# Row maxima moved from a PSUM bank into the tile of squares, with smaller edits ahead of the first expert

## The chip, the core and the metric

The program runs on one core of a Trainium2 chip. The core has a matrix engine (TensorE; PE in the rows, PEld for its weight loads), VectorE (DVE), ScalarE (ACT), GpSimd (POOL) and a queue engine, SyncE (SP), that issues the transfers. Each engine takes its own instructions strictly in order and waits on semaphores for the others. The metric is the device time of one execution in microseconds. The kernel before takes 633.98 us, the median of three runs (633.04 to 634.95).

## The reference

The reference chains three parts, all in float32.

Attention with random features, for 2 batches, 8 heads, 576 positions, head size 64 and 128 features:

```
def phi(x):
    proj = np.einsum('bhsd,md->bhsm', x, omega)
    sq = np.sum(x * x, axis=-1, keepdims=True) / 2.0
    h = proj - sq
    h = h - np.max(h, axis=-1, keepdims=True)
    return np.exp(h) / np.sqrt(m)
q_p, k_p = (phi(q_s), phi(k_s))            # q, k times 64 ** -0.25
kv = np.einsum('bhsm,bhsd->bhmd', k_p, v)
num = np.einsum('bhsm,bhmd->bhsd', q_p, kv)
den = np.einsum('bhsm,bhm->bhs', q_p, k_p.sum(2))[..., None] + 1e-06
```

Then the result, 1152 tokens of width 512, goes through a layer that sends each token to the one of 8 experts with the largest logit (two matrix products with a ReLU between, scaled by a softmax weight and a sigmoid). Last comes a layer in which all 4 experts are applied to every token and summed with given weights.

## The kernel before, in words

Every float32 product that matters is made of three passes: an operand is split into a rounded high part (a cast on ScalarE) and a low part (the difference, `split`, L89 to L91), and high times high, high times low and low times high add up in PSUM.

Attention is cut into 18 units: 16 of (kind k or q, batch b, half of the heads hh, pair of positions jp) and two "rest" units (kr, qr) for positions 512 to 575. The loop at L574 is a software pipeline over stages `st`. In the stage of unit `st`: unit st+1 is transposed on TensorE and split by ScalarE (`qTh`) and VectorE (`qTl`) (`stage_a`, L282); k units of stage st-2 are multiplied into `kv` (`kv_part`, L352); q units of st-2 are transposed (L382, "pt<-e") and copied to `qpT` (L385 on ScalarE, L387 on VectorE); q units of st-3 are multiplied with `kvs` (L400, into a bank `pnd`), divided (L403 to L406, `xn`), transposed again (L416, into the same bank) and split to `xh` and `xl` (L427, L428); and unit st is projected (`project`, L300, twelve matmuls) and given its exponentials (`stage_b`, L311), in two halves a = 0, 1. The matmuls and transposes of attention are chained by hand in this order (`pe`, L254), so that TensorE never runs ahead of a matmul that waits. On the other engines the build's scheduler sets the order, from the order of the code and from estimates of its own.

In `stage_b` the largest value of each row is reduced from PSUM (L324) into four words `mx` at the end of `kbank`. That is the one PSUM bank in which `kv` is accumulated too. Two small instructions (L328, L329) subtract the squares and add them again, so that the offset `nb` is rounded as in the reference, and ScalarE's exponentials read `nb`. The squares `sq` come from `squares` (L262): for the first unit on VectorE, for all others on GpSimd as a tree of adds (L274, L278).

After stage 6 `prep_late` (L232) makes constants for the routing: `fold`, `cmask`, `iota`, `iota1`, `rev`, `ue`, `uc`, and it splits the gate weights. `main_expert` (L461) finds the expert of most tokens of a batch from the gate logits; `E0` (L711) then loads that expert's weights by a dynamic index, and its first matrix is split in eight pieces, the lows alternating between GpSimd and VectorE. From there on the experts follow one another with TensorE as the engine that is busy throughout.

Of the kernel before, what the change touches and what calls it, by code (L numbers as in the profile page):

```python
# [23 lines left out]
NE, NE2, FF = 8, 4, 1024  # L24
# [15 lines left out]
def moe_stack(ctx, tc, q, k, v, omega, w_gate, w_ogate, mw1, mw2, dprobs, dw1, dw2, out):  # L40
    nc = tc.nc
    TT, STT, TS = nc.vector.tensor_tensor, nc.vector.scalar_tensor_tensor, nc.vector.tensor_scalar
# [4 lines left out]
    cp = ctx.enter_context(tc.tile_pool(name="cp", bufs=1))  # L47
# [6 lines left out]
    ps_n = ctx.enter_context(tc.tile_pool(name="ps_n", bufs=2, space=PSUM))  # L54
# [6 lines left out]
    ident = cp.tile([128, 128], F32, name="ident")  # L61
# [12 lines left out]
    grm = cp.tile([128, 4, NE], F32, name="grm")  # L74
    fold = cp.tile([128, 32], F32, name="fold")
    cmask = cp.tile([128, 4], F32, name="cmask")
    i32 = cp.tile([128, 32], I32, name="i32")
    iota = cp.tile([128, 32], F32, name="iota")
    iota1 = cp.tile([128, 32], F32, name="iota1")
    rev = cp.tile([128, NE], F32, name="rev")  # L80
    ue = cp.tile([128, 4, NE], F32, name="ue")
    uc = cp.tile([128, 4, NE], F32, name="uc")
# [59 lines left out]
    ap = pool_a.enter_context(tc.tile_pool(name="ap", bufs=2))  # L142
    G = H // 2
# [86 lines left out]
        nc.gpsimd.tensor_scalar(upper, upper, 0.0, None, op0=ALU.is_gt)  # L230

    def prep_late():  # L232
        TT(fold, ident[:, 0:32], ident[:, 32:64], op=ALU.add)
        TT(fold, fold, ident[:, 64:96], op=ALU.add)
        TT(fold, fold, ident[:, 96:128], op=ALU.add)
        nc.vector.tensor_reduce(cmask, ident.rearrange("p (c r) -> p c r", r=32), axis=AX.X, op=ALU.add)
        nc.gpsimd.iota(i32, pattern=[[1, 32]], base=0, channel_multiplier=0)
        nc.vector.tensor_copy(iota, i32)
        TS(iota1, iota, 1.0, None, op0=ALU.add)
        TS(rev, iota[:, 0:NE], -1.0, float(NE), op0=ALU.mult, op1=ALU.add)  # L240
        nc.vector.tensor_copy(ue, iota[:, 0:NE].unsqueeze(1).to_broadcast([128, 4, NE]))
        nc.vector.tensor_copy(uc, iota[:, 0:4].unsqueeze(2).to_broadcast([128, 4, NE]))
        nc.vector.memset(lgr, 0.0)
        split(wgh, wgl, wg)
        ds_ = cp.tile([128, 9], F32, name="ds_")
        nc.vector.tensor_reduce(ds_, dpr, axis=AX.X, op=ALU.add)
        TS(ds_, ds_, 1e-9, None, op0=ALU.add)
        nc.vector.reciprocal(ds_, ds_)
        TT(pb, dpr, ds_.unsqueeze(2).to_broadcast([128, 9, NE2]), op=ALU.mult)

    sq, st_a, st_e = {}, {}, {}
# [10 lines left out]
    def squares(kind, b, hh, eng):  # L262

        src = raw[kind, b, hh] if b < 2 else raw[kind, 2]
        x = src.rearrange("p h j d -> p (h j) d") if b < 2 else src
        n = x.shape[1]
        x2 = ap.tile([128, n, D], F32, tag="x2", name="x2")
        s = ap.tile([128, n], F32, tag="sq" + kind + ("r" if b == 2 else ""), name="sq")
        if eng is nc.vector:
            for h in range(0, n, 4):  # L270
                TT(x2[:, h:h + 4], x[:, h:h + 4], x[:, h:h + 4], op=ALU.mult)
                nc.vector.tensor_reduce(s[:, h:h + 4], x2[:, h:h + 4], axis=AX.X, op=ALU.add)
        else:
# [102 lines left out]
    def stage_cq(u):  # L376

        kind, b, hh, j = u
        e = heads(*u)
        ps = ps_t.tile([128, G, 128], F32, tag="pt", name="pt")  # L380
        for i in range(G):
            pe(nc.tensor.transpose(ps[:, i, :], e[i], ident))  # L382
        t = ap.tile([128, G, 128], F32, tag="qpT" if b < 2 else f"qpTr{hh}", name="qpT", bufs=4 if b < 2 else 1)
        if j % 2:
            nc.scalar.copy(t, ps)  # L385
        else:
            nc.vector.tensor_copy(t, ps)  # L387
        st_e["T", u] = t
# [185 lines left out]
    for st in range(-1, n + 6):  # L574
# [565 lines left out]
```

## Time and profile before

| what | value |
|---|---|
| median of three runs | 633.98 us |
| profiled execution | 633.71 us, its span 631.9 us, mean granted clock 0.986 |
| busy over the span: TensorE, VectorE, ScalarE, GpSimd | 591.9, 416.7, 257.7, 256.1 us |
| first 115 us: TensorE, VectorE, ScalarE, GpSimd | 84.1, 79.5, 63.7, 49.8 us |
| the other 517 us: TensorE, VectorE | 507.8, 337.2 us |

The page's shares are means over two unlike parts. Attention ends at about 115 us; in it no engine is busy all the time. Behind it TensorE is busy for 98% of the time. So the two parts are to be read apart, the first by who waits for whom, the second by TensorE alone.

### The profile page before, as it was taken

Reading aid. Unit: us, or ns where it says so; the run is one execution under the profiler, and the core shown is the slowest. Engines: PE = TensorE matmul, PEld = TensorE weight load, DVE = VectorE, ACT = ScalarE, POOL = GpSimd, SP = SyncE. Lnnn points to the kernel's source line nnn. Section 1 sums busy time; section 2 is a strip of 40 time slices with the busy share of each in tenths; the row PEclk is TensorE's granted clock in tenths of the full one; section 3 lists DMA queues with packets and bytes.
Section 4 is the critical chain, followed back from the end, with each engine's and each line's share of the span. In section 5 each row is a group of like instructions: output and inputs, shape, how many; then the busy total and the mean of one; then the engine's idle time right before and its main releaser. Section 6 shows DMA issues by size and latency. Waiting matters only on the chain.

```text
span 631.9 us, 11286 instructions
## 1 busy us (share of the span) xinstructions
PE 591.9 (94%) x4302; PEld 538.4 (85%) x4303; DVE 416.7 (66%) x939; ACT 257.7 (41%) x626; POOL 256.1 (41%) x301
## 2 busy tenths in 40 slices
PE   8776685999999999899999999999999999999996
PEld 7656674989978999889899899899898898998995
DVE  7696657688434478976666756667666666666564
ACT  5636556460323154445433343343343343442230
POOL 6983003050000001368646646645745745744220
PEclk9989898999999999899999999999999999999999
DMA  8613106303453302202202102202102101100004
GB/s 220 146 45 88 35 6 219 121 5 105 163 185 135 134 1 68 67 1 67 68 0 68 67 0 68 67 1 67 67 1 66 67 2 67 66 1 2 1 1 149
DMA packets 41241, 42.82 MB, mean 68 GB/s; under 512 B 14816, under 2 KB 29408, under 8 KB 41184
## 3 DMA queue, kind: packets, MB, share of 16 engines
q1 hardware_dynamic: 40896, 42.00, 21.0%
q8 instruction: 35, 0.57, 0.4%
q14 instruction: 22, 0.18, 0.1%
q10 hardware_dynamic: 288, 0.07, 0.0%
HBM read 37.34 MB, written 4.72 MB: 67 GB/s over the span
## 4 chain that ended last, share of the span: by engine, by line
PE 65%; DVE 2%; DMA 1%; issue 0%; ACT 0%; SPq 0%
PE po L634 10%; PE po L635 10%; PE po L636 10%; PE pp L634 9%; PE pp L636 9%; PE pp L635 9%; PE py L634 1%; PE py L636 1%; PE py L635 1%; DMA st<-in_moe_w_dram 1%; PE ph L636 1%; PE ph L635 1%; PE ph L634 1%; DVE wlo L91 1%; DVE xcl L91 0%
## 5 line engine op out<-in xcount | busy, mean ns | idle before, releaser
L91 POOL TENSOR_TENSOR wlo<-st,whi 128x512 fp32r<-128x512 f32 x96 | 116.5, 1235 | 233.5 <-ACT whi L90 228.8
L1085 DVE SCALAR_TENSOR_TENSOR oacc<-po,pb,oacc 128x512 f32<-128x512 f32 x135 | 100.0, 748 | 55.6 <-PE po L636 55.6
L90 ACT CAST whi<-st 128x512 fp32r<-128x512 f32 x120 | 67.8, 592 | 117.6 <-PE po L636 49.2
L634 PE MATMUL po<-whi,hh 128*128 128x512 f32 x288 | 112.4, 390 | 0.0
L635 PE MATMUL po<-wlo,hh 128*128 128x512 f32 x288 | 112.1, 389 | 0.0
L636 PE MATMUL po<-whi,hl 128*128 128x512 f32 x288 | 112.0, 389 | 0.0
L630 POOL TENSOR_TENSOR hl<-c,hh 128x320 fp32r<-128x320 f32 (+1 forms) x64 | 52.6, 822 | 87.4 <-ACT hh L629 74.8
L635 PE MATMUL pp<-xl,whi 128*128 128x320 f32 (+1 forms) x256 | 76.0, 297 | 0.0
L634 PE MATMUL pp<-xh,whi 128*128 128x320 f32 (+1 forms) x256 | 75.9, 297 | 0.0
L636 PE MATMUL pp<-xh,wlo 128*128 128x320 f32 (+1 forms) x256 | 75.9, 297 | 0.0
L636 PEld LDWEIGHTS po<-whi,hl 128*128 128x128 f32 x288 | 54.1, 188 | 11.2
L634 PEld LDWEIGHTS po<-whi,hh 128*128 128x128 f32 x288 | 54.2, 188 | 10.0
L635 PEld LDWEIGHTS po<-wlo,hh 128*128 128x128 f32 x288 | 54.1, 188 | 10.1
L1032 DVE TENSOR_TENSOR c<-u,pp 128x320 f32<-128x320 f32 (+1 forms) x96 | 43.4, 453 | 22.1 <-PE pp L636 21.7
L635 PEld LDWEIGHTS pp<-xl,whi 128*128 128x128 f32 x256 | 48.8, 191 | 1.3
L634 PEld LDWEIGHTS pp<-xh,whi 128*128 128x128 f32 x256 | 48.8, 191 | 1.2
L628 ACT ACTIVATE c<-c 128x320 f32<-128x320 f32 (+1 forms) x64 | 28.5, 445 | 51.7 <-DVE c L1032 50.9
L636 PEld LDWEIGHTS pp<-xh,wlo 128*128 128x128 f32 x256 | 48.8, 191 | 0.0
L625 DVE SCALAR_TENSOR_TENSOR hl<-c,hh 128x320 fp32r<-128x320 f32 (+1 forms) x64 | 45.0, 736 | 0.3
L336 ACT ACTIVATE e<-pj,nb 128x128 f32<-128x128 f32 x144 | 41.2, 378 | 8.2 <-DVE nb L329 8.2
L634 PE MATMUL pp<-xch,whi 128*128 128x320 f32 (+1 forms) x128 | 38.3, 300 | 1.2 <-DVE c L1032 1.2
L634 PE MATMUL ph<-xh,whi 128*128 128x288 f32 x128 | 38.2, 298 | 1.2 <-ACT dg L665 1.2
(265 smaller groups left out, 1335.5 us busy)
## 6 DMA issues: line engine op xcount, KB each, us to landing
st<-in_moe_w_dram SPq DMA_DIRECT2D x32, 512.0 KB, 4.2
st<-in_moe_w_dram SPq DMA_DIRECT2D x10, 1024.0 KB, 6.9
q<-in_q_dram SPq DMA_DIRECT2D x4, 512.0 KB, 4.6
v<-in_v_dram SPq DMA_DIRECT2D x16, 128.0 KB, 4.0
xs<-xn SPq DMA_DIRECT2D x16, 128.0 KB, 1.8
own<-in_moe_w_dram SPq DMA_DIRECT2D x2, 1024.0 KB, 6.7
out_dram<-oacc SPq DMA_DIRECT2D x8, 256.0 KB, 2.0
k<-in_k_dram SPq DMA_DIRECT2D x3, 512.0 KB, 4.0
```

The source lines that it names most:

```text
L90: nc.scalar.copy(hi, src)
L91: eng.tensor_tensor(lo, src, f32(hi), op=ALU.subtract)
L336: nc.scalar.activation(e[:, i // 2, i % 2], ps[:, i // 2, i % 2], AF.Exp, bias=nb[:, i // 2, i % 2:i % 2 + 1])
L625: STT(hl, src, 0.0, f32(hh), op0=ALU.max, op1=ALU.subtract)
L628: nc.scalar.activation(c, c, AF.Relu)
L630: nc.gpsimd.tensor_tensor(hl, c, f32(hh), op=ALU.subtract)
L634: nc.tensor.matmul(ps, sh_, mh, start=start, stop=False)
L635: nc.tensor.matmul(ps, sh_, ml, start=False, stop=False)
L636: nc.tensor.matmul(ps, sl_, mh, start=False, stop=stop)
L1032: TT(c, u, p, op=op)
L1085: STT(oacc[:, T], po, pc, oacc[:, T], op0=ALU.mult, op1=ALU.add)
```

## The change

The words of the maximum, of the square and of the offset now lie next to each other in SBUF: the tile `sq` has four words for each row: 0 minus the maximum, 1 the scaled square, 2 the sum of the two, 3 minus the scaled square. The maximum is reduced straight into word 0 with its sign turned, and two `tensor_reduce` instructions over pairs of neighbouring words give word 2 and then `nb`. `kbank` holds `kv` alone. On GpSimd every `squares` gets two more instructions that write words 1 and 3; on VectorE the first unit's scale is folded into the multiplication and one more reduce writes word 3.

The constants of `prep_late` are written as integers by five `iota` instructions on GpSimd and turned to float32 by one cast; `fold` is one reduce in place of three adds; the low part of the gate weights goes to GpSimd. In the stage loop `main_expert` comes behind the transposes of the q units. All eight lows of E0's first matrix are on GpSimd. The three-pass projection stays as it is.

```
-MXS = 8
...
-    i32 = cp.tile([128, 32], I32, name="i32")
-    iota = cp.tile([128, 32], F32, name="iota")
...
+    i32 = cp.tile([128, 136], I32, name="i32")
+    consts = cp.tile([128, 136], F32, name="consts")
+    iota, iota1, rev = consts[:, 0:32], consts[:, 32:64], consts[:, 64:72]
...
-        TT(fold, ident[:, 0:32], ident[:, 32:64], op=ALU.add)
-        TT(fold, fold, ident[:, 64:96], op=ALU.add)
-        TT(fold, fold, ident[:, 96:128], op=ALU.add)
+        nc.vector.tensor_reduce(fold, ident.rearrange("p (c r) -> p r c", r=32), axis=AX.X, op=ALU.add)
...
-        nc.vector.tensor_copy(iota, i32)
-        TS(iota1, iota, 1.0, None, op0=ALU.add)
-        TS(rev, iota[:, 0:NE], -1.0, float(NE), op0=ALU.mult, op1=ALU.add)
-        nc.vector.tensor_copy(ue, iota[:, 0:NE].unsqueeze(1).to_broadcast([128, 4, NE]))
-        nc.vector.tensor_copy(uc, iota[:, 0:4].unsqueeze(2).to_broadcast([128, 4, NE]))
+        for c, w, pattern, base in ((0, 32, [[1, 32]], 0), (32, 32, [[1, 32]], 1), (64, 8, [[-1, 8]], 8),
+                                    (72, 32, [[0, 4], [1, 8]], 0), (104, 32, [[1, 4], [0, 8]], 0)):
...
+        nc.vector.tensor_copy(consts, i32)
...
-        split(wgh, wgl, wg)
+        split(wgh, wgl, wg, nc.gpsimd)
...
-        s = ap.tile([128, n], F32, tag="sq" + kind + ("r" if b == 2 else ""), name="sq")
+        s = ap.tile([128, n, 4], F32, tag="sq" + kind + ("r" if b == 2 else ""), name="sq")
...
+            nc.vector.tensor_reduce(s[:, :, 3], s[:, :, 1:2], axis=AX.X, op=ALU.add, negate=True)
...
+            for i, f in ((1, hs), (3, -hs)):
+                nc.gpsimd.tensor_scalar(s[:, :, i], s[:, :, 0], f, None, op0=ALU.mult)
...
-        mx = kbank[:, m0:m0 + 4].rearrange("p (x c) -> p x c", x=2)
-        nc.vector.tensor_reduce(mx, ps, axis=AX.X, op=ALU.max)
+        nc.vector.tensor_reduce(s[..., 0], ps, axis=AX.X, op=ALU.max, negate=True)
...
-        STT(mx, s, -hs, mx, op0=ALU.mult, op1=ALU.add)
-        last_nb[0] = STT(nb, s, -hs, mx, op0=ALU.mult, op1=ALU.subtract)
+        nc.vector.tensor_reduce(s[..., 2], s[..., 0:2], axis=AX.X, op=ALU.add)
+        last_nb[0] = nc.vector.tensor_reduce(nb, s[..., 2:4], axis=AX.X, op=ALU.add)
...
-        for b, lg in logits:
-            gate_late[b] = (b, lg) + main_expert(b, lg, ps_n, "nd")
         done, turned = turned, []
...
+        for b, lg in logits:
+            gate_late[b] = (b, lg) + main_expert(b, lg, ps_n, "nd")
...
-    E0.load1(engs=(nc.gpsimd, nc.vector))
+    E0.load1()
```

What the edits do to the order is seen at three places. First TensorE in the stage of unit 12 (q of batch 1): the matmuls into `kv` and into `pnd`, before and then after. A name behind "waits" is the engine whose semaphore is waited for.

```order
L352 MATMUL kv<-v_120,e 64x65 [waits DMAHW7_49,DVE_49]
L352 MATMUL kv<-v_120,e 64x65
L352 MATMUL kv<-v_120,e 64x65 [waits DMAHW0_49]
...
L400 MATMUL pnd<-kvs,qpT 64x65 [waits PE_49]
L400 MATMUL pnd<-kvs,qpT 64x65 x7
L400 MATMUL pnd<-kvs,qpT 64x65 [waits DVE_49]
```

```order
L348 MATMUL kv<-v_116,e 64x65 [waits DMAHW7_49]
L348 MATMUL kv<-v_116,e 64x65
L348 MATMUL kv<-v_116,e 64x65 [waits DMAHW1_49]
...
L396 MATMUL pnd<-kvs,qpT 64x65 [waits DVE_49]
L396 MATMUL pnd<-kvs,qpT 64x65 x7
L396 MATMUL pnd<-kvs,qpT 64x65 [waits DVE_49]
```

The first `kv` matmul no longer waits for VectorE; the first `pnd` matmul, which had only its own engine ahead of it, now does.

Second, VectorE at the same place: the two halves of unit 11, the low part `qTl` of unit 13 and the two `xl` (L428 before, L424 after).

```order
L324 TENSOR_REDUCE kv<-pj 128x4 [waits PE_49]
L328 SCALAR_TENSOR_TENSOR kv<-sq,kv 128x4 [waits DVE_49]
L329 SCALAR_TENSOR_TENSOR nb<-sq,kv 128x4 [waits DVE_49]
L324 TENSOR_REDUCE kv<-pj 128x4 [waits DVE_49,PE_49]
L292 SCALAR_TENSOR_TENSOR qTl<-pt,qTh 128x512 [waits Activation_49]
L328 SCALAR_TENSOR_TENSOR kv<-sq,kv 128x4 [waits DVE_49]
L428 TENSOR_TENSOR xl<-pnd,xh 128x2x128 [waits Activation_49]
L329 SCALAR_TENSOR_TENSOR nb<-sq,kv 128x4 [waits DVE_49]
L428 TENSOR_TENSOR xl<-pnd,xh 128x2x128 [waits Activation_49]
```

```order
L321 TENSOR_REDUCE sq<-pj 128x2x2 [waits PE_49] x2
L324 TENSOR_REDUCE sq<-sq 128x2x2 [waits DVE_49] x2
L291 SCALAR_TENSOR_TENSOR qTl<-pt,qTh 128x512 [waits Activation_49]
L325 TENSOR_REDUCE nb<-sq 128x4 [waits DVE_49] x2
L424 TENSOR_TENSOR xl<-pnd,xh 128x2x128 [waits Activation_49] x2
```

The two maxima now stand next to each other, the small sums behind them, and no `xl` stands between a half's maximum and its `nb`.

Third, VectorE at unit 2, the rest of k, whose squares come from GpSimd (Pool).

```order
L292 SCALAR_TENSOR_TENSOR qTl<-pt,qTh 128x512 [waits Activation_49]
L328 SCALAR_TENSOR_TENSOR kv<-sq,kv 128x4 [waits DVE_49]
L329 SCALAR_TENSOR_TENSOR nb<-sq,kv 128x4 [waits DVE_49]
L324 TENSOR_REDUCE kv<-pj 128x4 [waits DVE_49,PE_49]
L328 SCALAR_TENSOR_TENSOR kv<-sq,kv 128x4 [waits DVE_49,Pool_49]
L329 SCALAR_TENSOR_TENSOR nb<-sq,kv 128x4 [waits DVE_49]
```

```order
L321 TENSOR_REDUCE sq<-pj 128x4 [waits PE_49,Pool_49]
L291 SCALAR_TENSOR_TENSOR qTl<-pt,qTh 128x512 [waits Activation_49]
L324 TENSOR_REDUCE sq<-sq 128x4 [waits DVE_49]
L321 TENSOR_REDUCE sq<-pj 128x4 [waits PE_49]
L325 TENSOR_REDUCE nb<-sq 128x4 [waits DVE_49]
```

The wait for GpSimd has moved from the small sum to the maximum itself, which writes the tile that GpSimd fills, and the low part `qTl` of the next unit, which stood ahead of it, now stands behind it.

## Rows read from the trace of the kernel before

**Rows 1.** Windows: stretch, then each engine's busy time, granted clock, DMA share, GB/s.
```profile
0.00:115.00 115.00, 84.11 (x979) 74.08 (x981) 79.48 (x231) 63.73 (x198) 49.81 (x85) 0.94 0.42 114
115.00:632.00 517.00, 507.78 (x3326) 464.33 (x3324) 337.21 (x709) 193.96 (x429) 206.26 (x216) 1.00 0.17 58
```

**Rows 2.** Waits of TensorE in 0 to 115: total us, times, longest.
```profile
PE kv L352 <- DVE nb L329: 14.0, 8, 2.3
PE pnd L416 <- DVE xn L406: 7.3, 3, 4.3
PE pt L382 <- DVE qTl L292: 4.5, 4, 1.3
```

**Rows 3.** Timeline of TensorE, unit 11 to unit 12: start, us, instruction [idle before].
```profile
65.41 0.39 PE L306 MATMUL pj<-omh,qTh 128*128 128x256 f32 x1
...
70.10 1.15 PE L352 MATMUL kv<-v,e 128*64 128x65 f32 x32 [2.13 <-DVE nb L329]
...
72.77 0.58 PE L306 MATMUL pj<-omh,qTh 128*128 128x256 f32 x1
```

**Rows 4.** Timeline of VectorE in the same stage.
```profile
66.55 0.69 DVE L324 TENSOR_REDUCE kv<-pj 128x4 f32<-128x512 f32 x1
...
69.56 0.42 DVE L428 TENSOR_TENSOR xl<-pnd,xh 128x256 fp32r<-128x256 f32 x1 [0.46 <-ACT xh L427]
69.90 0.15 DVE L329 SCALAR_TENSOR_TENSOR nb<-sq,kv 128x4 f32<-128x4 f32 x1
69.96 0.42 DVE L428 TENSOR_TENSOR xl<-pnd,xh 128x256 fp32r<-128x256 f32 x1
```

**Rows 5.** Groups by shape, 0 to 160: count, busy us, mean ns, idle before.
```profile
L324 DVE TENSOR_REDUCE kv<-pj 128x4 f32<-128x512 f32 x36 | 25.1, 696 | 11.0 <-PE pj L308 7.1 <-ACT kvs L373 1.9 <-PE pnd L416 0.5
L292 DVE SCALAR_TENSOR_TENSOR qTl<-pt,qTh 128x512 fp32r<-128x512 f32 x18 | 12.3, 685 | 1.7 <-ACT qTh L291 1.7
L91 POOL TENSOR_TENSOR wlo<-st,whi 128x512 fp32r<-128x512 f32 x8 | 11.4, 1431 | 44.6 <-ACT whi L90 44.6
L328 DVE SCALAR_TENSOR_TENSOR kv<-sq,kv 128x4 f32<-128x4 f32 x36 | 5.8, 160 | 1.5 <-POOL sq L278 0.6
```

**Rows 6.** Timeline of VectorE while the late constants are made.
```profile
32.20 0.45 DVE L233 TENSOR_TENSOR fold<-ident 128x32 f32<-128x32 f32 x1
32.57 0.27 DVE L236 TENSOR_REDUCE cmask<-ident 128x4 f32<-128x128 f32 x1
...
34.87 1.87 DVE L241 COPY ue<-iota 128x32 f32<-128x32 f32 x1
...
37.36 1.02 DVE L247 TENSOR_SCALAR ds__581<-ds__581 128x9 f32<-128x9 f32 x1
...
39.28 0.74 DVE L406 TENSOR_TENSOR xn<-pnd,rd 128x256 f32<-128x256 f32 x2
```

**Rows 7.** Timeline of TensorE: what waits for that, and two matmuls behind lows.
```profile
39.74 0.77 PE L416 MATMUL pnd<-ident,xn 128*128 128x128 f32 x4 [4.33 <-DVE xn L406]
...
104.56 0.44 PE L416 MATMUL pnd<-ident,xn 128*128 128x128 f32 x2 [1.74 <-DVE xn L406]
106.23 0.69 PE L416 MATMUL pnd<-ident,xn 128*128 128x128 f32 x2 [1.23 <-DVE xn L406]
```

**Rows 8.** Timeline of GpSimd and VectorE at unit 2.
```profile
15.34 0.19 POOL L278 TENSOR_TENSOR sq<-x 128x8 f32<-128x8 f32 x1
...
15.57 0.17 DVE L328 SCALAR_TENSOR_TENSOR kv<-sq,kv 128x4 f32<-128x4 f32 x1 [0.57 <-POOL sq L278]
```

**Rows 9.** Timeline of TensorE: the first two waits for nb.
```profile
17.18 1.15 PE L352 MATMUL kv<-v,e 128*64 128x65 f32 x32 [1.04 <-DVE nb L329]
...
21.69 1.15 PE L352 MATMUL kv<-v,e 128*64 128x65 f32 x32 [0.86 <-DVE nb L329]
```

**Rows 10.** Windows in which the granted clock is low, columns as in Rows 1.
```profile
72.00:75.00 3.00, 3.00 (x27) 2.88 (x24) 2.07 (x7) 0.00 (x0) 0.00 (x0) 0.55 0.25 86
...
102.00:113.00 11.00, 5.75 (x70) 4.84 (x70) 7.88 (x18) 7.19 (x19) 5.49 (x4) 0.69 0.62 191
```

More of the change, by code (lines that the diff above doesn't have):

```diff
@@ L76, in moe_stack @@
     cmask = cp.tile([128, 4], F32, name="cmask")
-    i32 = cp.tile([128, 32], I32, name="i32")
-    iota = cp.tile([128, 32], F32, name="iota")
[L79 to L82, printed above, removed]
+    i32 = cp.tile([128, 136], I32, name="i32")
+    consts = cp.tile([128, 136], F32, name="consts")
+    iota, iota1, rev = consts[:, 0:32], consts[:, 32:64], consts[:, 64:72]
+    ue, uc = (consts[:, c:c + 32].rearrange("p (c e) -> p c e", e=NE) for c in (72, 104))
     lgr = cp.tile([16, 128], F32, name="lgr")
@@ L232, in prep_late @@
     def prep_late():
-        TT(fold, ident[:, 0:32], ident[:, 32:64], op=ALU.add)
-        TT(fold, fold, ident[:, 64:96], op=ALU.add)
-        TT(fold, fold, ident[:, 96:128], op=ALU.add)
+        nc.vector.tensor_reduce(fold, ident.rearrange("p (c r) -> p r c", r=32), axis=AX.X, op=ALU.add)
         nc.vector.tensor_reduce(cmask, ident.rearrange("p (c r) -> p c r", r=32), axis=AX.X, op=ALU.add)
-        nc.gpsimd.iota(i32, pattern=[[1, 32]], base=0, channel_multiplier=0)
-        nc.vector.tensor_copy(iota, i32)
-        TS(iota1, iota, 1.0, None, op0=ALU.add)
-        TS(rev, iota[:, 0:NE], -1.0, float(NE), op0=ALU.mult, op1=ALU.add)
-        nc.vector.tensor_copy(ue, iota[:, 0:NE].unsqueeze(1).to_broadcast([128, 4, NE]))
-        nc.vector.tensor_copy(uc, iota[:, 0:4].unsqueeze(2).to_broadcast([128, 4, NE]))
+        for c, w, pattern, base in ((0, 32, [[1, 32]], 0), (32, 32, [[1, 32]], 1), (64, 8, [[-1, 8]], 8),
+                                    (72, 32, [[0, 4], [1, 8]], 0), (104, 32, [[1, 4], [0, 8]], 0)):
+            dst = i32[:, c:c + w]
+            nc.gpsimd.iota(dst if len(pattern) == 1 else dst.rearrange("p (a b) -> p a b", b=8),
+                           pattern=pattern, base=base, channel_multiplier=0)
+        nc.vector.tensor_copy(consts, i32)
         nc.vector.memset(lgr, 0.0)
-        split(wgh, wgl, wg)
+        split(wgh, wgl, wg, nc.gpsimd)
         ds_ = cp.tile([128, 9], F32, name="ds_")
@@ L267, in squares @@
         x2 = ap.tile([128, n, D], F32, tag="x2", name="x2")
-        s = ap.tile([128, n], F32, tag="sq" + kind + ("r" if b == 2 else ""), name="sq")
+        s = ap.tile([128, n, 4], F32, tag="sq" + kind + ("r" if b == 2 else ""), name="sq")
+        hs = SCALE * SCALE / 2
         if eng is nc.vector:
             for h in range(0, n, 4):
-                TT(x2[:, h:h + 4], x[:, h:h + 4], x[:, h:h + 4], op=ALU.mult)
-                nc.vector.tensor_reduce(s[:, h:h + 4], x2[:, h:h + 4], axis=AX.X, op=ALU.add)
+                STT(x2[:, h:h + 4], x[:, h:h + 4], hs, x[:, h:h + 4], op0=ALU.mult, op1=ALU.mult)
+                nc.vector.tensor_reduce(s[:, h:h + 4, 1], x2[:, h:h + 4], axis=AX.X, op=ALU.add)
+            nc.vector.tensor_reduce(s[:, :, 3], s[:, :, 1:2], axis=AX.X, op=ALU.add, negate=True)
         else:
@@ L276, in squares @@
             while w:
-                dst = x2[:, :, 0:w] if w > 1 else s.unsqueeze(2)
+                dst = x2[:, :, 0:w] if w > 1 else s[:, :, 0:1]
                 nc.gpsimd.tensor_tensor(dst, x2[:, :, 0:w], x2[:, :, w:2 * w], op=ALU.add)
                 w //= 2
+            for i, f in ((1, hs), (3, -hs)):
+                nc.gpsimd.tensor_scalar(s[:, :, i], s[:, :, 0], f, None, op0=ALU.mult)
         sq[kind, b, hh] = s
@@ L317, in stage_b @@
         if rest:
-            s = sq[kind, 2, 0][:, G * a:G * a + G].rearrange("p (x c) -> p x c", x=2)
+            s = sq[kind, 2, 0][:, G * a:G * a + G].rearrange("p (x b) c -> p x b c", x=2)
         else:
-            s = sq[kind, b, hh].rearrange("p (h j) -> p h j", j=4)[:, 2 * a:2 * a + 2, 2 * jp:2 * jp + 2]
+            s = sq[kind, b, hh].rearrange("p (h j) c -> p h j c", j=4)[:, 2 * a:2 * a + 2, 2 * jp:2 * jp + 2]
         e = ap.tile([128, 2, 2, M], F32, tag="e" if not rest else f"er{kind}{a}", name="e", bufs=EB if not rest else 1)
-        m0 = 512 - 4 * MXS + 4 * (flip[0] % MXS)
-        mx = kbank[:, m0:m0 + 4].rearrange("p (x c) -> p x c", x=2)
-        nc.vector.tensor_reduce(mx, ps, axis=AX.X, op=ALU.max)
+        nc.vector.tensor_reduce(s[..., 0], ps, axis=AX.X, op=ALU.max, negate=True)
         nb = ap.tile([128, 2, 2], F32, tag="nb", name="nb", bufs=4)
-        hs = SCALE * SCALE / 2
-        STT(mx, s, -hs, mx, op0=ALU.mult, op1=ALU.add)
-        last_nb[0] = STT(nb, s, -hs, mx, op0=ALU.mult, op1=ALU.subtract)
+        nc.vector.tensor_reduce(s[..., 2], s[..., 0:2], axis=AX.X, op=ALU.add)
+        last_nb[0] = nc.vector.tensor_reduce(nb, s[..., 2:4], axis=AX.X, op=ALU.add)
         flip[0] += 1
```

## The prediction, made before the changed kernel ran

> **What bounds the kernel now.** I read the windows first: they part the span at 115 us [rows 1]. Behind it TensorE is busy 507.8 of 517 us, and the change touches nothing that it does there, so that part keeps its length and only begins earlier or later. Ahead of it TensorE is busy 84.1 of 115 us and VectorE 79.5; neither is full, so waits between engines set the length, and the rest of the reading is in that stretch.
>
> The waits of TensorE come next [rows 2]. The largest is 14.0 us in eight waits, all of the same kind: a matmul into `kv` waits for VectorE to finish `nb`. It does not need `nb`. What `kv` multiplies are exponentials of two stages ago; the wait exists because `mx` lies in the bank that `kv` is written to. The timeline of one stage shows the price [rows 3, 4]: TensorE has been free since 67.97, VectorE ends the last `nb` at 69.90 + 0.15 = 70.05, the `kv` matmuls start at 70.10, and unit 12 is projected at 72.77, 7.36 us after unit 11. In that stage the last `nb` even stands behind an `xl` that waited for ScalarE.
>
> **The change part by part.** The sum is made against the profiled execution, 633.7 us, of which 631.9 is the span.
>
> *The bank (term 1).* In the order after, no `kv` matmul waits for VectorE. The first two of the eight waits, 1.04 and 0.86 [rows 9], I count at nothing: at unit 2 GpSimd now has two instructions more for the squares, four more `iota` and parts of another unit ahead of them, six or more of about 0.19 [rows 8], so the squares come 1.1 to 1.5 us later. VectorE waited 0.57 for them already, and now waits with the maximum itself, ahead of `qTl`. The six others are 14.0 - 1.9 = 12.1 us. What is late next? In the stage of rows 3, the first `pnd` matmul needs a bank that the `xl` of the stage read. Without the wait `kv` would be done by 67.97 + 1.1 = 69.1. VectorE, from 66.55 on, has two maxima (1.4), sums (0.3), `qTl` (0.69), sums (0.2) and two `xl` (0.8) [rows 4, 5]: about 69.9, against 70.38 before. So the second half of `pnd` starts at 69.9 and not at about 71.2 to 71.6; of the 2.13 some 1.3 is gained and 0.85 is not. Two of the six stages have two such `pnd` (units 12 and 16); in the others one short `pnd` follows, and the first `xl` lies beside `kv`. Term 1 is 12.1 - 2 x 0.85 = **10.4**. Bounds: 3.6 if only VectorE's own shorter chain counts (two halves cost about 2.5 us with their dependent steps before and 1.9 after, 0.6 x 6), 14.0 if nothing comes in its place.
>
> *The sums (term 2).* 72 small scalar_tensor_tensor of 0.16 us become 72 `tensor_reduce` of two words. No row has that shape. The bounds are 0.16 (L328, as many words written [rows 5]) and 0.27 (the reduce of 128 words, L236 [rows 6]). I take 0.16, the row nearest in words, so nothing; at 0.27 they add 72 x 0.11 = 7.9 us of VectorE, of which at most half lies on the chain, 4. The maximum reads the same 512 words of PSUM, 0.70, and only its four results go elsewhere: nothing.
>
> *The late constants (term 3).* Before, VectorE is at them from 32.20 to 39.28 [rows 6], and the transposes of `xn` behind them make TensorE wait 4.33 us [rows 7]. Up to 37.36 that is 5.16 us; in its place stand two reduces at 0.27, one cast of 136 words, a memset and a small reduce (0.3 together). The cast is between 0.16 and the 1.87 of the copy of 32 words. So 2.5 to 4.2 us are saved. I take **4.0**: the copy and the tensor_scalar of 1.02 are long because GpSimd was at work, and the reduce in the same stretch was not [rows 6]. The Trainium skill (SBUF — State Buffer, Who interferes with whom) says that VectorE's copies, casts and tensor_scalar in the two-port modes, and a tensor_tensor with both inputs in SBUF, contend with GpSimd for a port pair that one instruction holds to its end, and that a tensor_reduce never does on trn2; the trace agrees, 1.87 and 1.02 beside 0.27. By that rule the one cast may still meet a long GpSimd instruction, and term 3 would be 2.5.
>
> *E0's lows (term 4).* Four lows leave VectorE. Behind them TensorE waited 1.74 and 1.23 us for `xn` [rows 7], 2.97 together. The granted clock in that stretch was 0.69, with 5.75 us of TensorE busy [rows 10]; at full clock that is 1.8 less. I take a third of it, since ScalarE's casts and the wait for the transfer stay in the same stretch: 2.97 + 0.6 = **3.6**. Bounds 0 and 4.8.
>
> *The clock after the waits (term 5).* From 72 to 75 the granted clock was 0.55 [rows 10]: the lower level, 1.2 GHz, for nearly all of it, behind a TensorE that had waited 2.13 us in the stage before. With the wait shorter, 3.0 x 0.45 = 1.35 may come back; I take **1.2**, bounds 0 and 1.35.
>
> *What it costs (term 6).* In the four stages in which q units are transposed, TensorE waits for `qTl` (4.5 us in four [rows 2]). After, the 0.68 us copy to `qpT` stands ahead of `qTl` on VectorE in these; the adjacent maxima give back some of it. I take 0.5 each, 2.0, and 0.4 for the late squares at the start: **-2.4**, bounds 0 and -5.
>
> *The tail (term 7).* The eight lows in series on GpSimd take 8 x 1.43 = 11.4 us [rows 5] from the landing of the weights on, and the landing hangs on the gate of batch 0, which moves up less than the end of attention does. Before, all eight were done when attention ended. After, TensorE catches up with them, or with unit 17's exponentials behind the casts on ScalarE, for about one low: **-1.3**, bounds 0 and four lows, -5.7. Moving `main_expert` behind the transposes exchanges one short wait for another: nothing. The eight pairs of small GpSimd instructions later on lie where GpSimd is idle: nothing.
>
> Sum: 10.4 + 0 + 4.0 + 3.6 + 1.2 - 2.4 - 1.3 = 15.5 us. 633.7 - 15.5 = 618.2; the median of three lies 0.3 above the profiled execution, so the forecast is **618.5 us**.
>
> **The rivals.**
>
> *The wait comes back in another place.* Attention is a ring of TensorE, VectorE and ScalarE; with the `kv` wait gone, `pnd` waits for `xl`, the transposes for `qTl`, the projection for the exponentials that free its banks, in every stage and not in two. Then term 1 is its lower bound, 3.6, and term 5 goes with it: 3.6 + 4.0 + 3.6 - 2.4 - 1.3 = 7.5, 626.5 us. For it: VectorE is busy 79.5 of 115 us, and the first `pnd` matmul has a new wait for it. Against: in the stage that I followed row by row 1.3 of 2.13 stays.
>
> *Nothing comes in its place.* The losses of terms 1, 6 and 7 (1.9 + 1.7 + 2.4 + 1.3) do not show, since a TensorE that idles less also keeps its clock: 15.5 + 7.3 = 22.8, 611.2 us. Against: VectorE alone would then be busy some 70 of 92 us in a ring with many steps.
>
> *The sums are dear, and it is slower.* Each half has two `tensor_reduce` in a row between its maximum and its exponentials. If one of them costs 0.16 + y, the loss is up to 72 y, as far as all lie on the chain. It passes the gain at y = 15.5 / 72 = 0.22, and is slower by 0.3% at y = 17.4 / 72 = 0.24, a price of 0.40 us: 636 us. The Trainium skill speaks for it (VectorE: DVE Perf Modes, Rules for kernel authors): it calls `tensor_reduce` on a hot path the slowest VectorE operation and advises restructuring. The trace bears that out only for long rows: 0.70 for 512 words against 0.69 for a scalar_tensor_tensor of the same length is level [rows 5], and 128 words took 0.27.
>
> *It does nothing.* Another chain than attention sets when the experts start, 634 us. Against: the first expert's index comes out of attention's last stages, and TensorE is busy with attention until the experts begin.
>
> **How the numbers follow.** Chances: the forecast 0.64, the wait comes back 0.20, nothing in its place 0.09, dear sums 0.04, nothing happens 0.03. Below 0.3%, 1.9 us, a measurement of this kernel can't tell a change from none. All of the first three are faster: 0.93; no change 0.03 and slower 0.04. The range takes in both neighbours: 611 at the low end, and 628 at the high end for the returning wait with the dearer sums and term 3 at 2.5. The forecast's own range is 614 to 623.
>
> **What would show it.** Right: the `kv` wait for `nb` gone from TensorE's waits; attention done near 99 and not at 115; two `xn` waits behind the constants below 1.5 us; no VectorE lows for the first expert; the small reduces at 0.16 to 0.2. Wrong: `pnd` or the transposes waiting more than 8 us in total for `xl` or `qTl`; the granted clock low for longer than before; unit 2's maximum more than 3 us later; TensorE waiting for the first expert's lows.

## The result, and the profile after

The changed kernel takes **614.19 us**, the median of four runs (613.24 to 615.89). The kernel before took 633.51 beside it on the same chip (633.04 to 634.95): a ratio of 0.9694, 95% interval 0.9663 to 0.9725, so 19.3 us less. 618.5 us was forecast, with 614 to 623 as the forecast's own range; the result lies just inside its lower end. The profiled execution took 613.25 us, its span is 611.3 us: 20.6 us less than the span before, against 15.5 in the sum.

The windows of the kernel after, parted where attention ends; columns as in [rows 1]:

```profile
0.00:98.00 98.00, 83.92 (x1003) 74.25 (x1004) 67.97 (x225) 63.12 (x205) 58.47 (x111) 0.98 0.44 118
98.00:611.00 513.00, 504.54 (x3302) 459.75 (x3300) 336.67 (x704) 192.21 (x423) 207.68 (x218) 1.00 0.18 61
```

TensorE is busy 84 of 98 us, the last 3 of them for the first expert already, where it was 84 of 115; and the granted clock there is 0.98 where it was 0.94. The first expert's first matmul starts at 95.02 (before: 115.33), the first matmul of its second matrix at 119.29 (139.47), and 492 us follow in either kernel.

The waits of TensorE up to 98 us (what waited, on what: total us, times, longest), in answer to [rows 2]:

```profile
PE pt L378 <- DVE qTl L291: 2.8, 3, 1.2
PE pt L378 <- DVE qpT L383: 2.7, 3, 0.9
PE pj L307 <- DVE qTl L291: 2.6, 2, 2.4
PE pj L305 <- ACT e L332: 2.2, 2, 1.2
PE pnd L396 <- DVE xl L424: 1.2, 3, 0.4
...
PE pnd L412 <- DVE xn L402: 0.6, 1, 0.6
```

The 14.0 us of `kv` for `nb` are gone, and of the 7.3 for `xn` 0.6 is left. The stage of [rows 3] reads now, in TensorE's timeline:

```profile
59.46 0.39 PE L305 MATMUL pj<-omh,qTh 128*128 128x256 f32 x1
...
61.97 1.15 PE L348 MATMUL kv<-v,e 128*64 128x65 f32 x32
63.54 1.15 PE L396 MATMUL pnd<-kvs,qpT 128*64 128x65 f32 x32 [0.42 <-DVE xl L424]
64.62 0.39 PE L305 MATMUL pj<-omh,qTh 128*128 128x256 f32 x1
```

5.16 us from unit 11 to unit 12 and not 7.36; in place of 2.13 us for `nb`, 0.42 for `xl`. The groups of VectorE up to 98 us, in answer to [rows 5]:

```profile
L321 DVE TENSOR_REDUCE sq<-pj 128x4 f32<-128x512 f32 x36 | 24.2, 689 | 12.8 <-PE pj L307 7.8 <-POOL sq L278 4.6
...
L324 DVE TENSOR_REDUCE sq<-sq 128x4 f32<-128x8 f32 x36 | 5.4, 156 | 0.1
L325 DVE TENSOR_REDUCE nb<-sq 128x4 f32<-128x8 f32 x36 | 5.2, 154 | 0.1
```

The new sums take 0.155 us each, as forecast. The 4.6 us of idle time in the first row are one wait, at unit 2: the maximum now writes into the tile of squares and waits for GpSimd, which finished them late, at 18.15 and not at 15.53 [rows 8]. That maximum in VectorE's timeline, before and then after, and what TensorE then waits for at unit 3, after:

```profile
14.29 0.70 DVE L324 TENSOR_REDUCE kv<-pj 128x4 f32<-128x512 f32 x1
```

```profile
18.19 0.69 DVE L321 TENSOR_REDUCE sq<-pj 128x4 f32<-128x512 f32 x1 [4.62 <-POOL sq L278]
```

```profile
19.53 0.39 PE L307 MATMUL pj<-omh,qTl 128*128 128x256 f32 x1 [2.39 <-DVE qTl L291]
```

Unit 4 is projected at 25.87; before it was 22.78. So the gain was made although the start lost 3.1 us. Two more windows, in answer to [rows 10]:

```profile
22.00:25.90 3.90, 3.90 (x45) 3.50 (x44) 1.78 (x6) 1.79 (x7) 3.36 (x8) 0.58 0.77 250
64.60:69.40 4.80, 4.80 (x81) 4.45 (x77) 4.03 (x14) 2.96 (x11) 0.00 (x0) 1.00 0.19 58
```

The low clock (0.58) now stands at the start, behind TensorE's waits of 2.39 and 1.18 at unit 3; in the stage of unit 12 it is 1.00.

### The profile page after: what moved, and what is told of

The parts are those of the page before. It is cut to its first block, busy times and chain, and to the rows that moved or that the text cites. A ratio compares the mean times of both kernels' runs of the same rounds, so it can differ in the third digit from the quotient of the medians.

```text
span 611.3 us, 11277 instructions
## 1 busy us (share of the span) xinstructions
PE 588.5 (96%) x4302; PEld 534.0 (87%) x4303; DVE 404.6 (66%) x929; ACT 255.3 (42%) x626; POOL 266.2 (44%) x328
## 4 chain that ended last, share of the span: by engine, by line
PE 66%; DVE 3%; DMA 1%; issue 1%; ACT 0%; SPq 0%
PE po L630 11%; PE po L632 11%; PE po L631 11%; PE pp L630 9%; PE pp L632 9%; PE pp L631 9%; PE py L630 1%; PE py L632 1%; PE py L631 1%; DMA st<-in_moe_w_dram 1%; PE ph L631 1%; PE ph L630 1%; PE ph L632 1%; DVE wlo L88 1%; DVE xcl L88 1%
## 5 line engine op out<-in xcount | busy, mean ns | idle before, releaser
L88 POOL TENSOR_TENSOR wlo<-st,whi 128x512 fp32r<-128x512 f32 x100 | 120.6, 1228 | 218.5 <-ACT whi L87 216.7
L332 ACT ACTIVATE e<-pj,nb 128x128 f32<-128x128 f32 x144 | 39.3, 396 | 5.6 <-DVE nb L325 5.5
```

## The experiments

The table has the time at which TensorE starts the first projection of a unit, from the timelines of the profiled executions; "expert" is the first expert's first matmul, "second" the first of its second matrix. The names of the runs are those below. The stage of a unit is here the time from this start to that of the next unit.

| unit | before | after | e1 | e5 | e12 | e6 | e10 |
|---|---|---|---|---|---|---|---|
| 4 | 22.78 | 25.87 | 23.75 | 24.29 | 24.59 | 22.68 | 22.54 |
| 6 | 33.28 | 35.98 | 41.11 | 42.10 | 34.60 | 32.69 | 32.41 |
| 7 | 44.15 | 41.26 | 48.86 | 49.93 | 41.27 | 38.42 | 37.68 |
| 16 | 101.12 | 87.58 | 98.09 | 97.39 | 87.90 | 84.72 | 84.02 |
| 17 | 112.61 | 92.24 | 102.16 | 102.84 | 92.06 | 89.51 | 88.74 |
| expert | 115.33 | 95.02 | 104.2 | 106.3 | 93.9 | 92.3 | 91.5 |
| second | 139.47 | 119.29 | 131.2 | 131.2 | 119.7 | 116.6 | 115.8 |

Ratios are to the kernel before, run beside each; gains in us are differences of these medians. The build's scheduler orders VectorE's instructions anew for every kernel, so a run can differ from its neighbour in more than the lines shown.

### The bank alone (e1)

```
-        m0 = 512 - 4 * MXS + 4 * (flip[0] % MXS)
-        mx = kbank[:, m0:m0 + 4].rearrange("p (x c) -> p x c", x=2)
+        mx = ap.tile([128, 2, 2], F32, tag="mx", name="mx", bufs=8)
```

> The kernel before with one edit: the words of the maxima lie in an SBUF tile of their own instead of the bank of kv; the two scalar_tensor_tensor sums, the constants and the lows of the first expert stay as before. Theory (the shared bank held TensorE): the kv waits for nb, 14.0 us, are gone, and attention ends 11 to 14 us earlier, since the squares are no later than before; 620 to 623 us. Rival (the gain of the change comes from the work that it takes off VectorE, and the wait comes back as pnd and transposes waiting for xl and qTl): 628 us or more.

Measured: 624.26 us, ratio 0.984 (0.9812 to 0.9868), 9.9 us gained, between the two expectations. No `kv` matmul waits for VectorE any more, and from unit 7 to the expert 15.8 us are saved (55.3 for 71.2). But units 4 to 7 cost 25.1 us for 21.4. VectorE's groups up to 105 us show a price that neither side had foreseen:

```profile
L327 DVE SCALAR_TENSOR_TENSOR mx<-sq,mx 128x4 f32<-128x4 f32 x34 | 11.0, 333 | 0.2
L328 DVE SCALAR_TENSOR_TENSOR nb<-sq,mx 128x4 f32<-128x4 f32 x34 | 10.0, 306 | 0.1
```

The same instructions took 160 ns while `mx` lay in PSUM [rows 5]. With `mx` in SBUF the means are 333 and 306, about twice that.

### The form of the sums (e5)

```
-        nc.vector.tensor_reduce(s[..., 2], s[..., 0:2], axis=AX.X, op=ALU.add)
-        last_nb[0] = nc.vector.tensor_reduce(nb, s[..., 2:4], axis=AX.X, op=ALU.add)
+        TT(s[..., 2], s[..., 0], s[..., 1], op=ALU.add)
+        last_nb[0] = TT(nb, s[..., 2], s[..., 3], op=ALU.add)
```

> The changed kernel with its two sums as tensor_tensor adds of the same SBUF words instead of tensor_reduce. Theory (an instruction of VectorE with both inputs in SBUF is held up by GpSimd's squares, a tensor_reduce is not): the adds take 0.3 us or more in the mean and not 0.155, VectorE is busy 10 us longer in attention, unit 7 is projected 3 us later or more; 617 to 622 us. Rival (the form of the sum doesn't matter, and what the bank alone did not give lies in the constants and the lows): 0.16 us in the mean, 613.5 to 615 us.

Measured: 625.81 us, ratio 0.988 (0.985 to 0.991), slower than the upper end expected. In the code only the form of 72 instructions of four words differs from the changed kernel, and 11.1 of its 19.3 us are lost. The scheduler also set some twenty of VectorE's instructions at units 2 to 5 in another order, and what that alone is worth isn't shown. Unit 4 is projected earlier than in the changed kernel; the loss lies behind it. Units 4 to 7 took 25.6 us for 15.4, with VectorE busy 21.3 of them and the granted clock at 0.80 for 1.00. The rows of VectorE, then of GpSimd, in the same stretch (start, duration):

```profile
23.36 1.91 DVE L325 TENSOR_TENSOR nb<-sq 128x4 f32<-128x4 f32 x1
...
27.63 1.64 DVE L324 TENSOR_TENSOR sq<-sq 128x4 f32<-128x4 f32 x1
29.19 0.68 DVE L321 TENSOR_REDUCE sq<-pj 128x4 f32<-128x512 f32 x1
```

```profile
23.35 1.89 POOL L271 TENSOR_TENSOR x<-k 128x1024 f32<-128x1024 f32 x1
25.32 2.07 POOL L275 TENSOR_TENSOR x<-x 128x512 f32<-128x512 f32 x2
27.35 1.89 POOL L271 TENSOR_TENSOR x<-q 128x1024 f32<-128x1024 f32 x1
```

An add of four words that starts beside a GpSimd multiplication ends with it: 23.36 + 1.91 = 25.27 and 23.35 + 1.89 = 25.24; 27.63 + 1.64 = 29.27 and 27.35 + 1.89 = 29.24. Beside two GpSimd instructions of 0.28, from 22.71 on, the adds at 23.04 and 23.16 took 0.20 and 0.17. Up to 110 us 21 adds took more than 0.25, and each of them ended 0.01 to 0.03 us behind the end of a GpSimd instruction. In the changed kernel 32 of the reduces lay wholly within a GpSimd instruction of 0.5 us or more, and the longest of them took 0.17. VectorE's groups up to 105 us have the means, against 156 and 154 ns for the reduces of the changed kernel among the same GpSimd work:

```profile
L325 DVE TENSOR_TENSOR nb<-sq 128x4 f32<-128x4 f32 x34 | 13.1, 396 | 0.1
...
L324 DVE TENSOR_TENSOR sq<-sq 128x4 f32<-128x4 f32 x34 | 10.8, 328 | 0.1
```

The Trainium skill (SBUF — State Buffer, Who interferes with whom) says that a VectorE instruction with two SBUF inputs contends with a GpSimd instruction that reads SBUF, one with at most one SBUF input outside the two-port modes does not, and a tensor_reduce on trn2 never does; the trace agrees in all three: 0.31 to 0.40 with two inputs in SBUF, 0.16 with one of them in PSUM, 0.155 as a reduce.

### The bank back (e2), and the maxima by themselves (e12)

The changed kernel with the maxima in `kbank` and the sums as scalar_tensor_tensor:

```
-        nc.vector.tensor_reduce(s[..., 0], ps, axis=AX.X, op=ALU.max, negate=True)
+        m0 = 480 + 4 * (flip[0] % 8)
+        mx = kbank[:, m0:m0 + 4].rearrange("p (x c) -> p x c", x=2)
+        nc.vector.tensor_reduce(mx, ps, axis=AX.X, op=ALU.max)
...
+        STT(mx, s[..., 1], -1.0, mx, op0=ALU.mult, op1=ALU.add)
+        last_nb[0] = STT(nb, s[..., 1], -1.0, mx, op0=ALU.mult, op1=ALU.subtract)
```

> The changed kernel with the maxima back in words of the kv bank, and the two sums as scalar_tensor_tensor again; squares, constants, main_expert and lows stay as changed. Theory: the kv waits come back, 11 to 13 us, 625 to 627 us; what is left of the gain, 7 to 8 us, is the constants and the lows. Rival (the other edits carry the gain): 618 us or less.

Measured: 628.59 us, ratio 0.9907 (0.9877 to 0.9937): 5.6 us gained of 19.3. The other edits leave a little less than expected.

The opposite: the kernel before with the changed `squares` and `stage_b`, and all else as it was. The lines of the change's diff that it has:

```
+        s = ap.tile([128, n, 4], F32, tag="sq" + kind + ("r" if b == 2 else ""), name="sq")
...
+        nc.vector.tensor_reduce(s[..., 0], ps, axis=AX.X, op=ALU.max, negate=True)
...
+        nc.vector.tensor_reduce(s[..., 2], s[..., 0:2], axis=AX.X, op=ALU.add)
+        last_nb[0] = nc.vector.tensor_reduce(nb, s[..., 2:4], axis=AX.X, op=ALU.add)
```

> The kernel before with the maxima, the squares' four words and the two tensor_reduce sums of the change, and nothing else: old constants, old place of main_expert, lows of the first expert on both engines. Theory (free bank and sums in a form that GpSimd does not hold up carry the whole gain): 611 to 613.5 us, attention done near 92 us. Rival (the lows and the place of main_expert carry a part that the runs so far hide): 616 us or more.

Measured: 613.99 us (609.99 to 614.09, two of six runs near 610), 0.5 above the range expected, ratio 0.9664 (0.9632 to 0.9695): 19.6 us gained, as much as by the whole change. The late constants and the lows of the first expert, 7.6 us of the forecast's 15.5, add nothing to it.

### The late constants (e14 on the kernel before, e6 on the changed one)

On the kernel before, `prep_late` and the tiles of the change, as its diff has them:

```
-        nc.vector.tensor_copy(iota, i32)
...
+        nc.vector.tensor_copy(consts, i32)
...
+        split(wgh, wgl, wg, nc.gpsimd)
```

> The kernel before with the late constants of the change, and nothing else. By term 3 of the prediction 4.0 us are gained in the stage of unit 6: 630 us. Theory from the opposite edit on the changed kernel (which gained 2 us): the stage gains 3 to 5 us, the four more iota instructions hold up the squares of unit 2 by 0.5 to 2 us; 630.5 to 633 us. Rival: no gain in the stage either, 633 to 635 us.

Measured: 631.47 us, ratio 0.9966 (0.9945 to 0.9988), 2.1 us gained. The stage of unit 6 took 6.47 us for 10.87: 4.4 saved, as term 3 has it; 1.3 went in the next stage (7.79 for 6.53) and 0.5 at the start.

On the changed kernel, the old constants, the same lines the other way round:

```
-        nc.vector.tensor_copy(consts, i32)
...
+        nc.vector.tensor_copy(iota, i32)
...
+        split(wgh, wgl, wg)
```

> The changed kernel with the late constants made on VectorE as before. Term 3 of the prediction: 4.0 us are lost, all of them in the stage in which unit 6 is projected (5.28 us long in the changed kernel): 618 to 619 us. Rival (the stage costs more, since its small instructions also meet GpSimd's squares): 5 to 6 us, 619.5 to 620.5 us. Other rival (the wait is taken up later in the ring): 615 us or less.

Measured: 612.13 us, ratio 0.9674 (0.9638 to 0.9709). Nothing is lost; 2.5 us more are gained than by the change, though the intervals overlap. The stage of unit 6 took 5.73 us for the changed kernel's 5.28, and unit 4 came 3.2 us earlier: with four `iota` fewer on GpSimd, VectorE's wait for the squares of unit 2 is 2.6 us and not 4.6. Part of the 3.2 is the clock. The windows from 20 to 26 us, first of the changed kernel and then of this run:

```profile
20.00:26.00 6.00, 4.82 (x50) 4.22 (x49) 3.38 (x12) 3.65 (x13) 5.30 (x10) 0.72 0.55 169
```

```profile
20.00:26.00 6.00, 5.30 (x66) 4.83 (x65) 4.00 (x13) 4.49 (x17) 5.29 (x10) 1.00 0.64 200
```

At a granted clock of 0.72, 4.82 us of TensorE are, by an estimate from this row, 1.3 us more than at 1.00. The old constants, then, had not been long in themselves. GpSimd's row in the kernel before, beside VectorE's copy `ue` in [rows 6]:

```profile
34.80 1.91 POOL L274 TENSOR_TENSOR x<-q 128x1024 f32<-128x1024 f32 x1
```

The copy of 32 words that took 1.87, from 34.87 to 36.74, ended 0.03 us behind that multiplication. With the maxima alone (e12) the same copy and the cast, in VectorE's timeline, fell among GpSimd's short instructions, and only `pb` met a long one:

```profile
33.62 0.23 DVE L241 COPY ue<-iota 128x32 f32<-128x32 f32 x1
...
35.17 1.71 DVE L249 TENSOR_TENSOR pb<-dpr,ds__590 128x36 f32<-128x36 f32 x1
```

```profile
33.56 0.24 POOL L280 TENSOR_TENSOR x<-x 128x32 f32<-128x32 f32 x1
...
34.94 1.89 POOL L276 TENSOR_TENSOR x<-k 128x1024 f32<-128x1024 f32 x1
```

### The lows of the first expert (e7 and e8)

On the kernel before, all eight on GpSimd:

```
-    E0.load1(engs=(nc.gpsimd, nc.vector))
+    E0.load1()
```

> The kernel before with the lows of the first expert all on GpSimd, and nothing else. By term 4 of the prediction 3.6 us are gained, in the stage of unit 16: 630 us. Rival (as in the changed kernel the edit is worth nothing): 633 to 634.5 us. If 630 is measured here and nothing was lost by the opposite edit on the changed kernel, the two gains overlap: the same stage, shortened once.

Measured: 630.03 us, ratio 0.9941 (0.9913 to 0.9969): 3.55 us gained (2.0 to 5.5 by the interval), where term 4 had 3.6, and in its stage (unit 16 to 17 8.11 us for 11.49). The same edit undone on the changed kernel:

```
-    E0.load1()
+    E0.load1(engs=(nc.gpsimd, nc.vector))
```

> The changed kernel with the lows of the first expert alternating between GpSimd and VectorE again. By term 4 of the prediction the two waits for xn come back, 2.5 to 3.6 us, in the stage of unit 16: 616.7 to 618 us. Theory from the run with the bank alone (its stage of unit 16 was short, 4.07 us, with these lows on VectorE, and 2.9 us were lost later): the stage stays under 5.5 us and 2 to 3 us are lost between the first matmul of the first expert and its second matrix; 616 to 617.5 us. Rival (the lows are hidden either way): 613.5 to 615 us.

Measured: 614.54 us, ratio 0.9706 (0.9667 to 0.9745): nothing lost. The stage of unit 16 takes 4.71 us with the lows on VectorE. What changed is VectorE's order there. Before, a low stood ahead of `xn`, and waited 1.67 for ScalarE; in this run, and in the run with the maxima alone, whose rows are shown, the lows stand behind both `xn`:

```profile
102.82 1.35 DVE L91 TENSOR_TENSOR wlo<-st,whi 128x512 fp32r<-128x512 f32 x1 [1.67 <-ACT whi L90]
104.09 0.41 DVE L406 TENSOR_TENSOR xn<-pnd,rd 128x256 f32<-128x256 f32 x1
```

```profile
87.97 0.42 DVE L407 TENSOR_TENSOR xn<-pnd,rd 128x256 f32<-128x256 f32 x1
...
88.70 0.42 DVE L407 TENSOR_TENSOR xn<-pnd,rd 128x256 f32<-128x256 f32 x1
...
91.85 1.54 DVE L91 TENSOR_TENSOR wlo<-st,whi 128x512 fp32r<-128x512 f32 x2
```

The first pair is the kernel before, the second the run with the maxima alone. The weights arrive about 0.5 to 1.1 us after unit 16's projection has begun in both (first cast at 101.64 and 89.02), so it is the order and not the arrival. With the lows on VectorE again the expert starts earlier, at 93.56 and not at 95.02, and takes as much longer to its second matrix, 25.8 us for 24.3: that one comes at 119.38 and 119.29.

### How much room VectorE has (e4)

```
-        nc.vector.tensor_reduce(s[..., 2], s[..., 0:2], axis=AX.X, op=ALU.add)
+        for _ in range(2):
+            nc.vector.tensor_reduce(s[..., 2], s[..., 0:2], axis=AX.X, op=ALU.add)
+        nc.vector.tensor_reduce(nb, s[..., 2:4], axis=AX.X, op=ALU.add)
         last_nb[0] = nc.vector.tensor_reduce(nb, s[..., 2:4], axis=AX.X, op=ALU.add)
```

> The changed kernel with the first of the two sums of every half done twice: 36 more tensor_reduce of 4 words on VectorE, between the maximum and the exponentials. At 0.16 us each that is 5.8 us of VectorE. Theory (VectorE's chain from the projection to the exponentials is part of the ring): at least a third of it shows, 616 to 619 us. Rival (VectorE has slack in every stage): within 1 us of the changed kernel, 614 to 615 us. A third reading, that these reduces are dear (0.27 or more each), would be seen in their rows, and give 620 us or more.

The kernel that ran repeats both sums and not only the first, 72 more reduces and not 36, 11 us of VectorE. Measured: 618.08 us (614.21 to 619.11), ratio 0.9726 (0.9697 to 0.9755), 3.2 us less gained than by the change. The reduces keep their 0.155 us. 3.5 us are lost in the stage of unit 6 alone (8.81 for 5.28), where VectorE now met long GpSimd instructions in two rows of the constants (1.87 and 1.07); the stages of units 7 and 17 lost 1.1 and 1.0, and unit 4 came 0.8 earlier. The nine stages from unit 8 to unit 17 take 46.26 us for 45.92: with the bank free VectorE has room there for the 0.6 us that each of them got.

### The start (e3, e10, e11)

The squares of the k rest on VectorE:

```
+            with tc.issue_after(last_nb[0].ins):
+                return squares(kind, 2, 0, nc.vector)
```

> The changed kernel with the squares of the k rest on VectorE, behind the first unit's offsets, instead of on GpSimd. Theory (the late squares of unit 2 held the start back): VectorE's wait of 4.6 us for them is gone, unit 4 is projected 2.5 to 3.5 us earlier than in the changed kernel, and that stays to the end: 611 to 612 us. Rival (the ring swallows it: another wait, for the next squares on GpSimd or for the transfers of k and q, takes its place): 613.5 to 615 us.

Measured: 612.82 us, ratio 0.9667 (0.9644 to 0.9691), which can't be told from the changed kernel. The wait of 4.6 is gone and unit 4 comes at 22.98, 2.9 earlier; 1.4 is given back in the stage of unit 6 (6.66 for 5.28), where `ds_` and `pb` took 1.38 and 1.09.

Then the constants ahead of the first projection, `pb` behind attention, and GpSimd's squares of the k rest ahead of those of the first q:

```
+    prep_slots()
+    prep_early()
...
+            with tc.issue_after(last_sq["k", 2].ins):
+                squares(kind, b, hh, nc.gpsimd)
...
+        prep_pb()
```

> The changed kernel with three things moved: the constants (and the slot numbers) are made while VectorE and GpSimd wait for the first transfers, the normalised domain weights pb behind attention, and GpSimd does the squares of the k rest ahead of those of the first q, not interleaved with them. Theory (the late squares cost 2.8 us at unit 2, and VectorE's work in the stage of the constants is on the path): VectorE's wait of 4.6 us is gone, unit 4 is projected near 23, unit 7 near 37.5 to 39 and not at 41.26, attention ends 2.5 to 4 us earlier; 610 to 612 us. Rival (the stages before unit 8 are set by the transfers or by GpSimd's other squares): 613 to 615 us.

Measured: **609.65 us** (608.68 to 611.21), ratio 0.9619 (0.9592 to 0.9647), 24.3 us gained, a little more than expected; the interval lies below that of the changed kernel. Units 4 and 7 came where expected. Unit 1, however, was projected at 11.76 and not at 9.50. The last run puts `fold`, `cmask` and the cast behind the second unit's offsets.

```
-    prep_early()
+    prep_iotas()
...
+        if st == 2:
+            with tc.issue_after(last_nb[0].ins):
+                prep_early()
```

> The kernel of the early constants with one thing put elsewhere: fold, cmask and the cast stand behind the second unit's offsets on VectorE, not ahead of the first projection. Theory: unit 1 is projected near 9.5 and not at 11.76, and all later units 1.5 to 2.5 us earlier: 607 to 608.5 us. Rival (the squares of the first q on GpSimd set unit 3, whatever stands ahead): 609 to 610.5 us.

Measured: 610.04 us, ratio 0.9618 (0.9592 to 0.9644), and unit 1 at 11.55: the theory fell. The windows from 6.6 to 11.5 us, first of the changed kernel and then of this run, show where the 2 us are:

```profile
6.60:11.50 4.90, 3.59 (x27) 3.18 (x27) 4.21 (x11) 2.23 (x8) 3.09 (x3) 1.00 1.07 245
```

```profile
6.60:11.50 4.90, 4.38 (x19) 3.98 (x20) 3.58 (x11) 0.44 (x1) 3.73 (x9) 0.65 1.26 264
```

The granted clock is 0.65 where it was 1.00, so a good part of the stretch ran at the lower level, 1.2 GHz. TensorE had waited 0.40 for `qTh`, 0.31 for `oml` and 0.21 for `qTl` ahead of it; in the changed kernel it was 0.40 and 0.22. What brings the clock down here is left open.

## Why the prediction was right in the time and wrong in the parts

By stages of the two profiled executions, the 20.6 us come together as follows; the forecast's terms are sorted into the same places.

| place | forecast | measured |
|---|---|---|
| five stages with a `kv` wait (units 7, 8, 11, 12, 15): terms 1, 5 | 10.2 | 9.7 |
| stage of unit 16: rest of term 1, term 4 | 5.0 | 6.8 |
| stage of unit 6: term 3 | 4.0 | 5.6 |
| other stages from unit 4 on: term 6 | -2.0 | +1.4 |
| start to unit 4: term 6 | -0.4 | -3.1 |
| behind unit 17: term 7 | -1.3 | +0.2 |

That the time came out inside the range is partly luck: the start lost 2.7 us more than forecast, all the other places together gained 7.8 us more, and the two errors cancel in part.

*Term 1, the bank,* was right where it was followed row by row: 33.6 us in the five stages became 23.9. What came in its place was 0.4 and not 0.85, in the two stages with two `pnd` (units 11 and 15 as counted here, 12 and 16 in the prediction). Its bound of 14.0 for "nothing comes in its place" was too low, though: the maxima and sums alone, without the other edits, gain 19.6. This is the step that failed. The prediction took each wait for the property of its own stage and priced it once. But the waits for `xn` at unit 6 and unit 16 were not made by the constants and the lows alone; when the bank is free, VectorE's order and its place beside GpSimd change, and these waits shrink with the constants and the lows as they were: these two stages took 6.67 for 10.87 and 4.16 for 11.49 in that run.

*Terms 3 and 4* were sized well for the kernel before: 4.4 us in its stage (2.1 in the end) and 3.55 us. On top of term 1 they are worth nothing in the end: the new constants still shorten the stage of unit 6 (5.28 for 6.67 with the maxima alone), but unit 4 comes 1.3 us later. Measured one at a time, the maxima with their sums, the constants and the lows make 19.6 + 2.1 + 3.55 = 25.2; together they make 19.3. With the bank shared (e2) the other edits gain 5.6, as much as constants and lows do by themselves; so it is the gain of the free bank that theirs overlaps with.

*Term 2, the sums,* has the right number, 0.155 us, and missed its meaning. Their form is not a detail of equal price: it is what lets the words lie in SBUF. With adds 11.1 us of the gain go. The prediction asked whether GpSimd holds up the cast of term 3, and did not ask it of 72 instructions whose second input moves from PSUM into SBUF. The rival of dear sums leaned on another sentence of the Trainium skill (VectorE: DVE Perf Modes, Rules for kernel authors), that a tensor_reduce on a hot path is the slowest operation; here the measurement differs, and it decides: 0.155 for the reduce and 0.33 to 0.40 for the tensor_tensor in its place. The rows that the prediction set beside that sentence, 0.70 and 0.69 for 512 words, were level too and did not bear it out.

*Term 5* can't be told from term 1 in these stages; the granted clock in the stage of unit 12 is 1.00, against the 0.55 of [rows 10].

*Term 6* erred twice. The start lost 3.1 and not 0.4: the prediction had the squares 1.1 to 1.5 later, and they were 2.6 later. VectorE began unit 2's first maximum at 18.19 and not at 14.29, 3.9 later and so beyond the 3 that the prediction had named as a sign of a wrong step, and everything behind it on VectorE, `qTl` of unit 3 too, came later with it. The four stages in which q units are transposed lost nothing, 19.4 us for 19.8: in three of them TensorE now waits for `qpT` and not for `qTl`, 0.9 each, and in the fourth 1.2 for `qTl`.

*Term 7* was -0.1: 24.3 us from the expert's first matmul to its second matrix, 24.1 before.

*The rivals.* "The wait comes back elsewhere" is refuted: in `pnd` and the transposes together TensorE waits 1.2 us for `xl` and 2.8 for `qTl`, where the prediction had put the sign of it at more than 8. "Nothing comes in its place" (611.2) lies 3.0 us below the measurement, the forecast 4.3 above it, and the mechanism of that rival is the nearer one, less the late start.

The runs leave three things open. The first is why one kernel's times fall on two values 4 us apart (the maxima alone, 610 and 614). The granted clock goes with them, 0.998 and 0.999 over the span near 610 and 0.993 to 0.996 near 614, and the profiled execution, at 613.99, had 0.72 from 20 to 26 us; what brings it down in one execution and not in another isn't shown. The second is which of VectorE's small instructions meets a long one of GpSimd in a given execution; the traces show the price, up to 1.9 us each time. The third is whether the shared bank or only the shared tile `kbank` makes the wait, for no run parts the two.

## What to carry to other kernels

Here words that TensorE never read made it wait 14.0 us, because they lay in the PSUM bank that it accumulates in; look for waits between instructions that exchange no data. When such words move to SBUF, count the SBUF inputs of every VectorE instruction that reads them: beside GpSimd's long instructions an add with two of them took up to 1.91 us here, a tensor_reduce over neighbouring words 0.155 in the mean. And where several waits lie on one ring of engines, price them together: what each edit gains alone is not what it adds.

## What the runs showed of the hardware that was not expected

Four words added by VectorE took 1.91 us when both inputs lay in SBUF and GpSimd had just begun a multiplication of 1.89 us; the mean over attention was 0.33 to 0.40 us (e5) against 0.155 for a tensor_reduce (the changed kernel) and 0.16 for a scalar_tensor_tensor with one input in PSUM (the kernel before). In the run with the k rest on VectorE (e3) two scalar_tensor_tensor of 256 words with both inputs in SBUF took 2.55 us together, beside GpSimd's multiplication and adds, where one takes 0.42 in the changed kernel.
